# The end of a matmul-bound kernel: the last inner product in two half-width banks, and other ways out for the last block's quarters

## The chip, the core and the metric

The kernel runs on one core of one Trainium2 chip. The metric is the device time of one execution in microseconds. Float32 goes in and comes out, and all matrix products run in float32.

## The reference

```python
batch, n_heads, seq, head_dim = (4, 8, 768, 64)
mask = q_bucket[:, :, :, None] == k_bucket[:, :, None, :]      # 6 sign bits of q @ proj and of k @ proj
scores = scale * np.matmul(q, k.transpose(0, 1, 3, 2))
scores = np.where(mask, scores, -1000000000.0)
attn = softmax(scores)                                         # max, exp, divide by the sum + 1e-9
x = np.matmul(attn, v) as (B*S, H*D) = (3072, 512)
h = x @ w_in                                                   # 512 -> 2048
g = np.maximum(h, 0.0) ** 2
return g @ w_out                                               # 2048 -> 512, float32
```

## The kernel before

The kernel has two parts. Attention over the 32 heads, taken in pairs, fills the first 310 us or so and leaves x, transposed, in device memory. Then come three chunks of 1024 tokens each. A chunk goes through `hidden` or `hidden_pair` (x times `w_in`, then the squared ReLU) and then through `project` (times `w_out`), both with features on the partitions and tokens in the columns.

The matrix products are done with seven products of half-size blocks in place of eight, and `project` does this on two levels. Its outer loop runs over k = 0 to 6. For each k, `product` runs the inner seven: `add(to, a, b, first, last)` issues four matmuls of 128 x 128 weights and 256 columns (w = 256, n = 4) into the bank `acc[to]`. A float32 matmul stands in the trace as two passes, each with a weight load of its own, so one `add` shows as eight MATMUL and eight LDWEIGHTS records. Three banks are used. `acc[0]` is a running sum: ScalarE copies it out (`keep`) as `one`, `two` and `three` on its way, while later products add on to it. The four results, c11, c12, c21 and c22, go to VectorE (`add_to`, line 1306), which adds them up to blocks of the output.

The functions `first_` to `fourth` say what is done with the results of outer product k. The last one, k = 6, is `fourth`. It closes the block (ih, jh) = (1, 0), features 256 to 511 of the first 512 tokens of the chunk, in four quarters n = 0 to 3. Quarter n has row n // 2 (128 features) and column n % 2 (256 tokens). In the last chunk this is the last work of the kernel, and `product` is called there with `last`. The order in which the quarters close is then 0 (c11), 3 (c22), 1 (c12), 2 (c21). So "the second quarter" is n = 1, "the fourth quarter" n = 3, and the one that closes last is n = 2.

A quarter has features on its partitions and has to leave with tokens in the rows. There are two ways out:

- `put_part` (quarters 0, 3 and 1): VectorE transposes 32 x 32 blocks (line 1337), and four stores write 32 features each, 256 runs of 128 bytes (line 1341). `LATE` names the queue of each store: quarter 0 has three on GpSimd and one on SyncE, quarter 3 four on ScalarE, quarter 1 three on SyncE and one on ScalarE.
- `put_last` (quarter 2): TensorE transposes 128 x 128 (line 1356), VectorE copies the first half out of PSUM (line 1360), ScalarE the second (line 1358), and two stores write 128 runs of 512 bytes each (line 1361), the first on SyncE, the second on ScalarE.

Stores that `put_part` issues are listed in `late`. At the end, TensorE and VectorE each wait for `late[-1]` before they go on:

```python
for engine in nc.tensor, nc.vector:
    tc.add_manual_dep(engine.nop().ins, late[-1].ins.name, SYNC)
```

Behind that, every engine tests a flag (`tc.If`, line 1604) and branches past `general`, a slow path that is not taken with these inputs. Then SyncE waits in turn for every semaphore (line 1779), and two rounds of barriers end the kernel.

Instructions run on each engine in the order in which they are written. The framework gives each DMA of SyncE's and ScalarE's queues one of eight semaphores. A DMA is issued only when the DMA before it on the same semaphore has landed, and that wait stands on the issuing engine's queue. Tiles of one name share a few buffers: two each for the PSUM tiles `acc0`, `acc1` and `acc2`, five for the SBUF tiles `h` (`NH`), in which the transposed quarters are stored from.

Of the kernel before, what the change touches and what calls it, by code (L numbers as in the profile page):

```python
# [8 lines left out]
FP32 = mybir.dt.float32  # L9
# [25 lines left out]
def kernel(  # L35
# [10 lines left out]
    nc = tc.nc  # L46
# [6 lines left out]
    P = 128  # L53
# [12 lines left out]
    NCH = 1024  # L66
    NCHUNK = B * S // NCH
# [3 lines left out]
    ident = glob.tile([P, P], FP32, name="ident")  # L71
# [9 lines left out]
    HF, HD, NR, NQ = DFF // 2, DM // 2, NFF // 2, NFF // 4  # L81
# [623 lines left out]
    for pr in range(NIN, NP):  # L705
        n = 2 if pr % 2 else int(pr not in (NP // 2, NP - 2))
# [30 lines left out]
    with tc.manual_schedule():  # L737
# [180 lines left out]
        p_r = fast.enter_context(tc.tile_pool(name="p_r", bufs=2, reuse_waits="tile"))  # L918
        p_k = fast.enter_context(tc.tile_pool(name="p_k", bufs=1, reuse_waits="tile"))
        ps_m = fast.enter_context(tc.tile_pool(name="ps_m", bufs=2, space=PSUM, reuse_waits="tile"))  # L920
        HN, QN, NH = NCH // 2, NCH // 4, 5
# [6 lines left out]
        flags = []  # L928
        KEPT = dict(one=2, two=1, three=2, five=1)

        def product(n, w, at, bt, c11, c12, c21, c22, hook=None, last=False):

            acc = [ps_m.tile([P, 512], FP32, name=f"acc{i}")[:, 0:w] for i in range(3)]

            def add(to, a, b, first, last):
                for i in range(n):
                    nc.tensor.matmul(  # L940
                        out=acc[to], lhsT=a(i), rhs=b(i), start=first and i == 0,
                        stop=last and i == n - 1, skip_group_check=True,
                    )

            def keep(of, name):
                t = p_r.tile([P, 512], FP32, name=name, bufs=KEPT[name])[:, 0:w]
                nc.scalar.copy(out=t, in_=acc[of])  # L947
                return t

            add(0, at(0), bt["11"], True, False)  # L950
            one = keep(0, "one")
            add(1, at(1), bt["21"], True, True)
            if hook:
                hook()
            c11(acc[1], one)
            if last:
                flags.append(nc.values_load(slow))
            add(0, at(4), bt["t2"], False, False)
            two = keep(0, "two")
            add(2, at(3), bt["t1"], True, False)  # L960
            five = keep(2, "five")
            add(0, at(5), bt["t3"], False, False)
            three = keep(0, "three")
            add(2, at(6), bt["22"], False, True)
            if last:
                c22(three, five)
            c12(acc[2], two)
            if not last:
                c22(three, five)
            add(0, at(2), bt["t4"], False, True)  # L970
            c21(acc[0])

# [329 lines left out]
        def block(t, n):  # L1302
            return t[:, n]

        def add_to(out, one, two):
            nc.vector.tensor_tensor(out=out, in0=one, in1=two, op=ALU.add)  # L1306
# [20 lines left out]
                    in_=ot[a * 32:(a + 1) * 32].rearrange("i (c j) -> i c j", j=32),  # L1327
                )

        LATE = {0: (nc.gpsimd,) * 3 + (nc.sync,), 3: (nc.scalar,) * 4, 1: (nc.sync,) * 3 + (nc.scalar,)}  # L1330
        late = []

        def put_part(n, o):

            row, col = n // 2, n % 2
            ot = p_r.tile([P, HN], FP32, name="h", bufs=NH)[:, 0:QN]
            nc.vector.transpose(out=ot, in_=o)
            lo = (NCHUNK - 1) * NCH + col * QN
            m0 = HD + row * P
            for a in range(P // 32):  # L1340
                late.append(LATE[n][a].dma_start(
                    out=out[lo:lo + QN, m0 + a * 32:m0 + (a + 1) * 32].rearrange(
                        "(c i) j -> i c j", i=32
                    ),
                    in_=ot[a * 32:(a + 1) * 32].rearrange("i (c j) -> i c j", j=32),
                ))

        def put_last(n, o):

            row, col = n // 2, n % 2  # L1350
            ot = p_r.tile([P, HN], FP32, name="h", bufs=NH)[:, 0:QN]
            lo = (NCHUNK - 1) * NCH + col * QN
            for t in range(QN // P):
                at = slice(t * P, (t + 1) * P)
                tp = ps_m.tile([P, 512], FP32, name=f"acc{t}")[:, 0:P]
                nc.tensor.transpose(out=tp, in_=o[:, at], identity=ident)
                if t:
                    nc.scalar.copy(out=ot[:, at], in_=tp)
                else:
                    nc.vector.tensor_copy(out=ot[:, at], in_=tp)  # L1360
                (nc.scalar if t else nc.sync).dma_start(
                    out=out[lo + t * P:lo + (t + 1) * P, HD + row * P:HD + (row + 1) * P],
                    in_=ot[:, at],
                )

        def project(i):

# [11 lines left out]
            def close(ih, jh, n):  # L1379
                o = outs[ih, jh, n // 2]  # L1380
                o[1] += 1
                if (i, ih, jh) == (NCHUNK - 1, 1, 0):
                    put = put_last if n == 2 else put_part
                    put(n, o[0][:, n % 2 * QN:(n % 2 + 1) * QN])
                elif o[1] == 2:
                    put_out(i, ih, jh, n // 2, o[0])

# [31 lines left out]
            def fourth(n, one, two):  # L1419
                add_to(out_block(1, 0, n), block(W, n), whole(one, two))  # L1420
                close(1, 0, n)

            more = i + 1 < NCHUNK
            uses = first_, seventh, fifth, third, second, sixth, fourth
            for k in range(7):
                b = OUTER[k][1]
                t1, t2 = tens.pop(k)
                if k == 0 and more:
                    load_x(i + 1)
                src = load_factor_units(k - 1) if i == 0 and 0 < k <= NQ else None  # L1430
                if k == 1 and src:
                    factor_units(0, src)
                if k == 2 and more:
                    sum_x(i + 1, 1)
                    sum_x(i + 1, 2)
                if i == 0 and k == NQ + 1:
                    load_peak(0)
                    load_peak(1)
                if k >= 5 and more:
                    load_inner(i + 1, 0, (k - 5,))  # L1440
                at = lambda m, k=k: lambda n: leaves[k, m][:, n]
                bt = {
                    "11": lambda n: b[:, n, 0:QN], "21": lambda n: b[:, NQ + n, 0:QN],
                    "22": lambda n: b[:, NQ + n, QN:HN], "t1": lambda n: t1[:, n],
                    "t2": lambda n: t2[:, n], "t3": lambda n: b[:, n, QN:HN],
                    "t4": lambda n: b[:, NQ + n, 0:QN],
                }

                def hook():
                    y21 = b[:, NQ:NR, 0:QN]  # L1450
                    minus(y21, y21, t2)
                    if k > 1 and src:
                        factor_units(k - 1, src)
                    if k == 5 and more:
                        sums_inner(i + 1, (2,))
                    if k + 1 < 7 and k not in (1, 3):
                        inner_sums(k + 1)
                    if k == 6 and more:
                        load_third_inner(i + 1, 0, nc.scalar)
                        sums_inner(i + 1, (0, 1))  # L1460

                counted = []

                def a_with_load(m, k=k):
                    load_leaf(7 * k + len(counted) + NLEAF - 2)
                    counted.append(m)
                    return at(m)

                use = uses[k]
                product(  # L1470
                    NQ, QN, a_with_load, bt, lambda *p: use(0, *p), lambda *p: use(1, *p),
                    lambda p: use(2, p, None), lambda *p: use(3, *p), hook,
                    (i, k) == (NCHUNK - 1, 6),
                )
                if k == 3 and more:
                    sum_x(i + 1, 3)
                    sum_x(i + 1, 4)
                if k == 4 and i + 1 == NCHUNK:
                    guard()
                if k == 0:  # L1480

                    for h in range(2):
                        at_h = slice(h * NQ, (h + 1) * NQ)
                        minus(b11[:, at_h], b22[:, at_h], b_t[:, at_h])
                    inner_sums(2)
                if k == 2:

                    for h in range(2):
                        at_h = slice(h * NQ, (h + 1) * NQ)
                        minus(b_t[:, at_h], b21[:, at_h], b11[:, at_h])  # L1490
                    inner_sums(4)
# [43 lines left out]
        for i in range(NCHUNK):  # L1535
            for s in range(NR):
# [9 lines left out]
                if i == 0 and r in THEN:  # L1546
                    m = THEN.index(r)
# [15 lines left out]
                for n in range(2):  # L1563
                    m = 2 * ((i - 1) * NR + s) + n
# [218 lines left out]
```

## Time and profile before

| | |
|---|---|
| median of 3 runs | 853.48 us (853.28 to 853.53) |
| the profiled execution | 853.88 us; its span, first to last instruction, 852.3 us |
| TensorE busy | 845.8 us, 99% of the span, granted clock 0.999 |
| VectorE, ScalarE, GpSimd busy | 88%, 47%, 20% |
| last matmuls of the last inner product | end at 846.75 us |
| last store issued | SyncE, 848.32 us |

Times in the timeline are counted from the span's start. The span is the part of the execution between the first and the last instruction that the profiler recorded; the execution's own time has 1.5 us more around it. SPq and ACTq are the queues of SyncE and ScalarE as far as they issue DMAs. PE is TensorE's matmul, PEld its weight load, DVE VectorE, ACT ScalarE, POOL GpSimd. "q8" and "q14" of kind "instruction" are the queues that fetch the engines' own code.

### The profile page before, as it was taken

The numbers are of one execution on the slowest core, as the hardware profiler recorded it, in microseconds if no ns is written. First come the engines' busy times: TensorE is split into PE (matmuls) and PEld (weight loads), VectorE is DVE, ScalarE is ACT, GpSimd is POOL, SyncE is SP. The second block draws the span as 40 slices with busy tenths as digits, with TensorE's granted clock in tenths as the row PEclk, the third lists the DMA queues.
The fourth block names the chain that finished last, engine by engine and source line by source line (L and its number), as shares of the span: only waits on it lengthen the run. The fifth ranks groups of instructions, "written<-read, shape, count | busy, mean of one in ns | idle before, by whom it ended". The sixth has DMA issues, their size and how long they took to land.

```text
span 852.3 us, 17018 instructions
## 1 busy us (share of the span) xinstructions
PE 845.8 (99%) x6594; PEld 542.3 (64%) x6594; DVE 746.6 (88%) x1023; ACT 400.9 (47%) x749; POOL 168.4 (20%) x283
## 2 busy tenths in 40 slices
PE   9999999999999999999999999999999999999997
PEld 4475444444485444444788866567888756568886
DVE  4898999999999998988999968888988788889776
ACT  5787777878777762222111145553111355541110
POOL 1321121303221201543122121111000311200003
PEclk9999999999999999999999999999999999999999
DMA  9976998989995517999977975537557865335566
GB/s 214 175 130 138 183 187 202 212 167 227 266 233 184 183 43 272 324 319 304 354 227 234 271 194 188 188 95 296 178 161 195 180 221 189 124 118 148 158 162 140
DMA packets 234230, 170.14 MB, mean 200 GB/s; under 512 B 164841, under 2 KB 193329, under 8 KB 234145
## 3 DMA queue, kind: packets, MB, share of 16 engines
q1 hardware_dynamic: 194384, 87.78, 42.2%
q0 software_dynamic: 16512, 42.45, 15.7%
q10 hardware_dynamic: 23248, 38.78, 14.8%
q8 instruction: 53, 0.87, 0.4%
q14 instruction: 33, 0.26, 0.1%
HBM read 127.15 MB, written 41.16 MB: 197 GB/s over the span
## 4 chain that ended last, share of the span: by engine, by line
PE 97%; DVE 1%; DMA 1%; ACT 0%; issue 0%; SPq 0%; ACTq 0%; POOL 0%; DVEq 0%; POOLq 0%
PE acc L940 39%; PE st L478 18%; PE xo L532 15%; PE acc L1204 13%; PE acc L1157 9%; PE tot L589 1%; PE hash L396 1%; DMA out_dram<-h 1%; PE tp L342 0%; PE xo L371 0%; DVE h L1320 0%; DVE o L1306 0%; PE hash L406 0%; PE xo L406 0%; DVE tmp L1306 0%; DVE sum L1306 0%
## 5 line engine op out<-in xcount | busy, mean ns | idle before, releaser
L484 ACT ACTIVATE e<-st 128x768 f32<-128x768 f32 x192 | 155.4, 810 | 56.4 <-PE st L478 52.2
L532 PE MATMUL xo<-e,v_nat 64*64 64x385 f32 (+1 forms) x1520 | 158.4, 483 | 0.0
L940 PE MATMUL acc<-b,leaf 128*128 128x256 f32 x600 | 133.0, 379 | 0.0
L940 PEld LDWEIGHTS acc<-b,leaf 128*128 128x128 f32 x600 | 113.9, 190 | 16.0 <-issue 0.5
L478 PE MATMUL st<-feat 64*64 64x384 f32 x1056 | 110.0, 482 | 0.0
L532 PEld LDWEIGHTS xo<-e,v_nat 64*64 64x64 f32 (+1 forms) x1520 | 62.1, 133 | 62.1 <-issue 50.1
L444 POOL DMA_DIRECT2D bits<-signed x120 | 62.5, 525 | 195.7 <-ACT signed L433 193.9
L1204 PE MATMUL acc<-t_x,w_unit 128*128 128x512 f32 x192 | 90.8, 595 | 0.0
L940 PE MATMUL acc<-t,leaf 128*128 128x256 f32 x336 | 75.9, 379 | 0.0
L940 PEld LDWEIGHTS acc<-t,leaf 128*128 128x128 f32 x336 | 63.8, 190 | 8.7
L1017 DVE SCALAR_TENSOR_TENSOR b<-h 128x512 f32<-128x512 f32 x96 | 65.7, 691 | 3.0
L478 PE MATMUL st<-bits 64*64 64x384 bf16 x768 | 67.9, 324 | 0.0
L520 DVE TENSOR_TENSOR total<-total,e 128x1536 f32<-128x1536 f32 x32 | 56.0, 1749 | 4.8 <-ACT e L484 3.9
L520 DVE TENSOR_TENSOR t_x<-t_x,e 128x1536 f32<-128x1536 f32 x32 | 55.9, 1747 | 4.3 <-ACT e L484 4.2
L940 PE MATMUL acc<-x,w_unit 128*128 128x512 f32 x128 | 56.5, 593 | 0.0
L478 PEld LDWEIGHTS st<-feat 64*64 64x64 f32 x1056 | 40.5, 133 | 25.1 <-issue 21.1
L947 ACT COPY two<-acc 128x256 f32<-128x256 f32 (+1 forms) x29 | 12.5, 431 | 88.0 <-PE acc L940 66.1
L940 PE MATMUL acc<-b_t,leaf 128*128 128x256 f32 x240 | 53.8, 379 | 0.0
L1204 PEld LDWEIGHTS acc<-t_x,w_unit 128*128 128x128 f32 x192 | 35.8, 190 | 26.7 <-issue 23.0
L1325 POOL DMA_DIRECT2D out_dram<-h x24 | 15.5, 655 | 181.6 <-DVE h L1320 181.6
L478 PE MATMUL st<-t_x 64*64 64x384 f32 x480 | 50.0, 482 | 0.0
L940 PEld LDWEIGHTS acc<-b_t,leaf 128*128 128x128 f32 x240 | 45.6, 190 | 6.2
(192 smaller groups left out, 1346.3 us busy)
## 6 DMA issues: line engine op xcount, KB each, us to landing
leaf<-w_out ACTq DMA_DIRECT2D x142, 256.0 KB, 3.1
raw<-in_moe_w_in_dram SPq DMA_DIRECT2D x8, 1024.0 KB, 6.1
raw<-in_moe_w_out_dram SPq DMA_DIRECT2D x8, 1024.0 KB, 7.2
w_unit<-w_in SPq DMA_DIRECT2D x16, 512.0 KB, 4.0
w_unit<-w_in SPq DMA_DIRECT2D x8, 896.0 KB, 8.8
w_out<-sums POOLq DMA_DIRECT2D x16, 448.0 KB, 7.5
v_nat<-in_v_dram SPq DMA_DIRECT2D x16, 384.0 KB, 5.1
x_all<-x_raw SPq DMA_DIRECT2D x16, 384.0 KB, 3.2
```

The lines of the kernel that those rows point to most:

```text
L396: nc.tensor.matmul(out=banks[g * NR_B:(g + 1) * NR_B, h, 0:HS], lhsT=projs[rows, h * D:h * D + NR_B], rhs=feat[pr][rows, w, c * HS:(c + 1) ...
L444: nc.gpsimd.dma_start(out=t[h * D:h * D + NBITS + 1, w, c * HS:(c + 1) * HS], in_=signed[pr % 2][at:at + NBITS + 1, h],)
L478: nc.tensor.matmul(out=st[k * HK:(k + 1) * HK, h, 0:HS], lhsT=src[1][rows, key], rhs=src[0][rows, cut], start=first, stop=not first, skip_ ...
L484: nc.scalar.activation(out=key_of(pr, kt)[:, :, i, 0:HS], in_=st[:, :, 0:HS], func=ACTF.Exp, scale=scale)
L520: nc.vector.tensor_tensor(out=totals[pr], in0=totals[pr], in1=e, op=ALU.add)
L532: return nc.tensor.matmul(out=outs[pr][h * D:(h + 1) * D, c, 0:HS + 1], lhsT=nat[pr, "v_nat"][rows, h, kt * D:(kt + 1) * D], rhs=key_of(pr ...
L940: nc.tensor.matmul(out=acc[to], lhsT=a(i), rhs=b(i), start=first and i == 0, stop=last and i == n - 1, skip_group_check=True,)
L947: nc.scalar.copy(out=t, in_=acc[of])
L1017: nc.vector.scalar_tensor_tensor(out=out, in0=h, scalar=0.0, in1=h, op0=ALU.max, op1=ALU.mult)
L1157: nc.tensor.matmul(out=out, lhsT=w(a), rhs=b, start=start, stop=stop, skip_group_check=True)
L1204: nc.tensor.matmul(out=to, lhsT=w[:, PLACE[a], f], rhs=bt[b](f), start=first and f == 0, stop=last and f == NFT // 2 - 1, skip_group_check ...
L1325: queue.dma_start(out=out[at, m0 + a * 32:m0 + (a + 1) * 32].rearrange("(c i) j -> i c j", i=32), in_=ot[a * 32:(a + 1) * 32].rearrange("i ...
```

## The change

It has three parts, all in the last outer product of the last chunk.

1. The last inner product (`at(2)` times `t4`) no longer adds on to `acc[0]`. It goes in two groups of 128 columns into two banks of its own (`halves`), 16 passes of 128 columns in place of 8 of 256. `acc[0]` is added to the block as soon as it is complete without it, and each half is added in an instruction of 128 columns of its own.
2. Quarter 1 (the second) leaves as quarter 2 does: through two transposes of TensorE, two copies (ScalarE's for quarter 1, VectorE's for quarter 2) and two stores of 512-byte runs. The four stores of both quarters are issued behind all four copies: SyncE, ScalarE for quarter 1, ScalarE, SyncE for quarter 2.
3. The four stores of quarter 3 (the fourth) go in turn to ScalarE's queue and SyncE's. Quarter 1 is no longer in `late`, so `late[-1]` is now the last store of quarter 3.

```diff
-            add(0, at(5), bt["t3"], False, False)
+            add(0, at(5), bt["t3"], False, bool(last))
...
+            if last:
+                halves = [ps_m.tile([P, 512], FP32, name=f"acc{m}")[:, 0:w // 2] for m in range(2)]
+                a = at(2)
+                for m, half in enumerate(halves):
+                    for i in range(n):
+                        nc.tensor.matmul(
+                            out=half, lhsT=a(i), rhs=bt["t4"](i)[:, m * w // 2:(m + 1) * w // 2],
+                            start=i == 0, stop=i == n - 1,
+                        )
+                return last(acc[0], halves)
             add(0, at(2), bt["t4"], False, True)
             c21(acc[0])
...
-        LATE = {0: (nc.gpsimd,) * 3 + (nc.sync,), 3: (nc.scalar,) * 4, 1: (nc.sync,) * 3 + (nc.scalar,)}
+        LATE = {0: (nc.gpsimd,) * 3 + (nc.sync,), 3: (nc.scalar, nc.sync) * 2}
...
-        def put_last(n, o):
+        turned_last = []
+
+        def turn_out(n, o, t, ot, name, copy, queue):
...
+            at = slice(t * P, (t + 1) * P)
+            lo = (NCHUNK - 1) * NCH + col * QN + t * P
+            tp = ps_m.tile([P, 512], FP32, name=name)[:, 0:P]
+            nc.tensor.transpose(out=tp, in_=o[:, at], identity=ident)
+            copy(out=ot, in_=tp)
+            return lambda: queue.dma_start(
+                out=out[lo:lo + P, HD + row * P:HD + (row + 1) * P], in_=ot
+            )
...
-                    put = put_last if n == 2 else put_part
-                    put(n, o[0][:, n % 2 * QN:(n % 2 + 1) * QN])
+                    o = o[0][:, n % 2 * QN:(n % 2 + 1) * QN]
+                    if n in LATE:
+                        put_part(n, o)
+                    else:
+                        turned_last.append((n, o))
...
+            def finish(one, halves):
+
+                fourth(2, one, None)
+                (_, o1), (_, o2) = turned_last
+                for t, half in enumerate(halves):
+                    at = slice(t * P, (t + 1) * P)
+                    add_to(o2[:, at], o2[:, at], half)
+                ot = p_r.tile([P, HN], FP32, name="h", bufs=NH)
+                stores = []
+                for t in range(4):
+                    n, o, copy = ((1, o1, nc.scalar.copy), (2, o2, nc.vector.tensor_copy))[t // 2]
+                    stores.append(turn_out(
+                        n, o, t % 2, ot[:, t * P:(t + 1) * P], ("acc2", "acc2", "acc1", "acc0")[t],
+                        copy, nc.scalar if t in (1, 2) else nc.sync,
+                    ))
+                for store in stores:
+                    store()
...
-                    (i, k) == (NCHUNK - 1, 6),
+                    finish if (i, k) == (NCHUNK - 1, 6) else None,
```

## The prediction

> **What bounds the kernel now.** I read the page first, then the chain of waits, then the end of the timeline.
>
> ```profile
> PE 845.8 (99%) x6594; PEld 542.3 (64%) x6594; DVE 746.6 (88%) x1023; ACT 400.9 (47%) x749; POOL 168.4 (20%) x283
> PE 97%; DVE 1%; DMA 1%; ACT 0%; issue 0%; SPq 0%; ACTq 0%; POOL 0%; DVEq 0%; POOLq 0%
> ```
>
> TensorE is the bound for 97% of the chain. The diff touches nothing ahead of the last seven-product of the last project step, so only what lies behind TensorE's last matmuls can move. The timeline of the end (start us, us):
>
> ```profile
> 843.78 2.97 PE L940 MATMUL acc<-b_t,leaf 128*128 128x256 f32 x13
> ...
> 845.52 0.42 DVE L1306 TENSOR_TENSOR o<-sum,tmp 128x256 f32<-128x256 f32 x1
> 845.98 0.45 DVE L1337 STREAM_TRANSPOSE h<-o 128x256 f32<-128x256 f32 x1
> 846.79 0.42 DVE L1306 TENSOR_TENSOR o<-sum,acc 128x256 f32<-128x256 f32 x1 [0.36 <-PE acc L940]
> ...
> 847.63 0.29 DVE L1360 COPY h<-acc 128x128 f32<-128x128 f32 x1 [0.42 <-PE acc L1356]
> 847.74 0.27 ACT L1358 COPY h<-acc 128x128 f32<-128x128 f32 x1 [4.03 <-DMA out_dram<-h]
> 848.03 0.35 ACTq L1361 DMA_DIRECT2D out_dram<-h  x1
> 848.32 0.39 SPq L1361 DMA_DIRECT2D out_dram<-h  x1
> ```
>
> Matmuls end at 846.75, the last add (it was waiting for them) at 847.21, its copy on VectorE at 847.92. SyncE's store could follow at 847.97 but starts at 848.32: its queue still holds second-quarter stores. SyncE's own waits and the DMA rows of 849.0 to 851.5 say what follows:
>
> ```profile
> SPq L1779 <- DMA out_dram<-h: 1.4, 1, 1.4
> ...
> SPq L1341 <- DMA out_dram<-h: 0.6, 1, 0.6
> ```
>
> ```profile
> q14 instruction: 3, 0.02, 3.8%
> q8 instruction: 1, 0.02, 2.5%
> ```
>
> The kernel's end waits 1.4 us for one store. It is SyncE's last (L1361): "DMA to landing" gives 1.7 for ScalarE's and 2.7 for SyncE's, so 848.32 + 2.69 = 851.01. Its landing records come 15 within 849.78 to 849.95 and one at 851.01. In between, one queue's packets stand still from 849.56 to 850.13, exactly until an instruction fetch (8 KB, 849.53, 0.61 us) ends. Such fetches follow each engine's final branch: ScalarE's 848.41 to 849.53, VectorE's 848.79 to 850.01, TensorE's 848.79 to 850.44 (16 KB, 0.98 us). So a fetch holds one ring, and behind the release (850.13) the landing takes another 0.88. After that come 1.32 us of final waits and barriers: 852.33. The execution took 853.88, 1.55 beyond its span; the other runs' median is 853.48, 0.40 less, so I apply the difference to 853.48.
>
> **The change part by part.**
>
> *Narrow last group.* Removed: 8 passes of 256 columns (0.216 apart, 844.86 to 846.75). Added: 16 passes of 128 columns with 16 weight loads. A pass's length grows 595 - 379 = 216 ns for 256 more columns, so 128 columns take 0.108; a weight load grows 190 - 133 = 57 ns for 64 more columns, so its own streaming is 0.114. A load starts as the matmul ahead of it starts, so I take the larger: 0.114. Ends: 0.108 (free) and 0.216 (no shorter than now). The first half then ends at 844.86 + 7 x 0.114 + 0.27 (a 128-column pass, L997's 272 ns) = 845.93, the second at 844.86 + 15 x 0.114 + 0.27 = 846.84, 0.09 late. New banks mean no wait for earlier readers: both buffers' last readers are of the product before.
>
> *VectorE's row.* Removed: the second quarter's 32x32 transpose (0.45) and the wide add behind the last matmul. Added: the wide add of acc[0] now goes early, at 845.98 to 846.40, in the place of that transpose; then an add of 128 columns for each half. These have no row; ends 0.42 (the wide add) and 0.29 (the 128x128 copy); I take 0.29, nearest in size. First: 846.44 to 846.73. Second: it waits for 846.84, runs 846.88 to 847.17; behind it only two copies are queued. Now: 847.21. So this part gains 0.04; at 0.42 an add it loses 0.11 (both adds then run back to back to 847.32), at 0.108 a pass it gains 0.12.
>
> *Second quarter through TensorE.* Removed: four stores of 256 runs of 128 B, three on SyncE and one on ScalarE (issue 0.32 to 0.45 each). Added: two TensorE transposes behind the 16 passes (846.69, 0.11 apart, done 847.13; they delay the last quarter's, ready at 847.22, by nothing), two ScalarE copies of 0.27 (847.06 and 847.36; they wait for TensorE, and behind them ScalarE has only its own two stores queued), two stores of 128 runs of 512 B: SyncE at 847.37, ScalarE at 847.66.
>
> *Fourth quarter on two queues.* ScalarE now issues four from 845.14, the last at 846.54, with its fifth at 847.09 to 847.51. After: two each from 845.14, done by 846.0. That clears both queues. SyncE is free from 847.7 instead of 848.21, so its stall of 0.6 (L1341, for a landing at 847.39) and the 0.35 of queueing go.
>
> *Last quarter.* Last add 847.17, transpose, and VectorE's copies (same 0.42 behind the add) 847.22 and 847.59 to 847.88. SyncE's store 847.93, against 848.32: 0.39 earlier. ScalarE's second store stands behind its first: 847.66 + 0.35 + 0.04 = 848.05, against 848.03. This one is now the last to be issued: 0.27 earlier than SyncE's was.
>
> *Landing.* Ends: 1.72 (ScalarE's row, undisturbed) gives 849.77, 1.24 before 851.01; 2.69 (SyncE's row) gives 850.74. What decides is the fetches, and the change moves them: TensorE's and VectorE's final branches wait for the last store in `late`. That was the second quarter's on ScalarE (landed 848.76, so both branched at 848.79); now it is the fourth quarter's on SyncE, issued about 845.53, landing 1.6 to 2.25 later (rows of L1341), 847.1 to 847.8. So both branches come a microsecond earlier, and their fetches with them. With 2.25 (its nearest row is the store of 845.14, in the same crowd) VectorE's fetch starts at 847.78 + 1.22 = 849.0 and TensorE's at 847.78 + 1.65 = 849.43. The last store's packets run 0.72 to 1.36 behind its issue (ScalarE's row): 848.77 to 849.41. VectorE's fetch lies in it; TensorE's just misses. Held until 849.0 + 0.36 to 0.61, take 849.5, and landing 0.88 behind: 850.37. Nothing else of the span changes. **Sum: 851.01 - 850.37 = 0.64 earlier: 853.48 - 0.64 = 852.8.**
>
> **The rivals.**
>
> *No fetch meets it.* For it: a fetch holds one ring of 16 and only what that ring has not yet sent, and ScalarE's last store, sent by 849.39, met none. Against: two fetches now fall around the last packets, and the one store of before that was sent late was caught. Then 1.24 is gained, and up to 0.36 more if the last landing's semaphore is the last one in SyncE's row of final waits (seven of 0.06 follow it now): 852.2, at best 851.9.
>
> *TensorE's long fetch meets it.* If the gating store lands at 847.5 instead, that fetch runs from 849.15 to 850.13, the very moment of the release now: landing 851.01, and the earlier issue buys nothing. 853.5.
>
> *Slower: a narrow pass costs as much as a wide one.* For it: no row has a float32 pass shorter than its 190 ns weight load outside the transposes. Against: at 256 columns the pitch is all columns, and loads overlap. At 0.216 the second half ends 844.86 + 15 x 0.216 + 0.27 = 848.37 and the last store goes out at 849.46; with 1.72 to 2.69 it lands at 851.18 to 852.15, 0.2 to 1.1 late: 853.7 to 854.6. It decides from a pitch of about 0.16 on, where the second half is 0.7 late and eats my 0.64. The Trainium skill ("TensorE: Matmul & The Clock Gate", Back-to-back issue gap) speaks for a mild form: streams of load and matmul at 128 columns space 81 ns against 56 for the matmul alone. No row here shows such passes in float32. An estimate from the page's figures, 25 ns more per pass (0.133), puts the second half 0.3 later than mine and the sum at 853.1.
>
> That the narrow halves don't overlap with the adds as meant is in the forecast already: the first half's add is off the path.
>
> **How the numbers follow.** Forecast 0.45 (own range 852.3 to 853.2: the fetch's 0.36 or 0.61, the add's ends), no fetch 0.23, TensorE's fetch 0.2, slow pass 0.09, else 0.03. 0.2% is 1.7 us, about what a measurement of this kernel can tell from no change; so nearly all cases lie within. Faster by more needs the no-fetch case's far end and a short landing (1.54 is the shortest row): 0.1. Slower by more needs the slow pass and a held ring, or what I haven't seen: 0.05. Range 851.8 to 854.2: leaves out the best end (0.08), the slow pass's upper part (0.05) and the rest (0.03).
>
> **What would show it.** Right: 16 narrow passes 0.11 apart in the last group; SyncE without a wait for a landing ahead of its last store; last issue near 848.0; TensorE's and VectorE's branches near 847.8 and one landing record of a last store about 0.6 behind the other 15. Wrong: narrow passes 0.16 or more apart, a last landing at 849.8 (no fetch) or 851 (the long one), or anything ahead of 843 that moved.

## The result, and the profile after

| | before | after |
|---|---|---|
| median | 853.43 us (852.30 to 855.26, 22 runs) | 854.93 us (853.66 to 856.83, 22 runs) |
| ratio, 95% interval | | 1.0016 [1.0010, 1.0022] |
| the profiled execution | 853.88 us, span 852.3 | 854.51 us, span 853.0 |
| last inner product's matmuls end | 846.75 us | 847.14 us |
| last store issued | 848.32 us | 848.26 us |
| last store landed | 851.01 us | 851.92 us |
| end of the span, behind the last of those matmuls | +5.58 us | +5.82 us |

The change makes the kernel 1.4 us slower (0.16%; 0.9 to 1.9 by the interval), where 0.6 us earlier was forecast. The time lies above the forecast's range, though within 0.2% of before.

Executions differ in when they reach their end, by stages long before it that the change doesn't touch: the last product ended at 846.14 us in one profile below and at 848.66 in another. So I compare tails: what follows the last matmul of the last inner product (846.75 before, 847.14 after). "+4.8" below means that many us behind it.

The page's busy times and its chain of waits:

```profile
PE 846.4 (99%) x6604; PEld 529.3 (62%) x6604; DVE 746.8 (88%) x1025; ACT 401.3 (47%) x750; POOL 167.7 (20%) x283
...
PE 99%; ACT 0%; DVE 0%; issue 0%; POOL 0%; POOLq 0%
```

TensorE is still the whole of the chain; the change put ten matmuls in (6604 against 6594). This chain ends with VectorE's last copy (848.18) and leaves out the stores behind it. What the change can move lies in the last product and behind it, so the end of the timeline is what to read (start us, us, engine and line, what it does, in brackets idle time and what ended it):

```profile
844.98 1.97 PEld L975 LDWEIGHTS acc<-b_t,leaf 128*128 128x128 f32 x16
...
845.20 1.95 PE L975 MATMUL acc<-b_t,leaf 128*128 128x128 f32 x16
...
845.47 0.82 SPq L1351 DMA_DIRECT2D out_dram<-h  x2
845.47 0.89 ACTq L1351 DMA_DIRECT2D out_dram<-h  x2
...
846.20 0.41 DVE L1316 TENSOR_TENSOR o<-sum,acc 128x256 f32<-128x256 f32 x1
846.72 0.29 DVE L1316 TENSOR_TENSOR o<-o,acc 128x128 f32<-128x128 f32 x1
...
846.98 0.87 PE L1366 MATMUL acc<-ident,o 128*128 128x128 f32 x4
847.18 0.29 DVE L1316 TENSOR_TENSOR o<-o,acc 128x128 f32<-128x128 f32 x1 [0.18 <-PE acc L975]
847.29 0.43 ACT L1367 COPY h<-acc 128x128 f32<-128x128 f32 x2 [3.25 <-DMA out_dram<-h]
847.51 0.67 DVE L1367 COPY h<-acc 128x128 f32<-128x128 f32 x2
...
847.75 0.85 ACTq L1368 DMA_DIRECT2D out_dram<-h  x2
847.81 0.83 SPq L1368 DMA_DIRECT2D out_dram<-h  x2
```

Sixteen narrow passes take 1.95 us, 0.112 apart. The last add, 0.29 us, starts 0.04 behind the last pass's end. The two copies of the second quarter on ScalarE and the two of the last on VectorE follow, and then two stores leave on each queue, the last at 848.26. This execution reached the last product 0.33 us later than the one before (its add at 844.53 against 844.20). With that taken off, VectorE's row holds within 0.1 us of the forecast, and ScalarE's two stores leave 0.24 and 0.16 earlier, as its two copies take 0.43 together and not one after the other. The groups by shape give the passes' mean length (busy us, mean ns):

```profile
L975 PE MATMUL acc<-b_t,leaf 128*128 128x128 f32 x16 | 1.9, 275 | 0.0
L975 PEld LDWEIGHTS acc<-b_t,leaf 128*128 128x128 f32 x16 | 1.9, 192 | 0.1
```

The loss is behind the last issue. The views give fetches and landings only as sums and ranges; the times of single ones, here and below, are read from the trace's own packet and semaphore records. SyncE's own waits from 840 to 853, then the instruction queues in the DMA rows of 849.0 to 850.7 (packets, MB, share), then the times from issue to landing of the four last stores (L1368):

```profile
SPq L1806 <- DMA out_dram<-h: 2.2, 1, 2.2
SPq L1368 <- DMA out_dram<-h: 1.5, 1, 1.5
```

```profile
q14 instruction: 3, 0.02, 7.1%
q8 instruction: 1, 0.02, 5.3%
```

```profile
DMA to landing us min/median/max: 1.8/2.7/3.7
```

L1806 is the final wait (L1779 before): it now stands 2.2 us where it stood 1.4. The first two of the four stores landed 1.75 and 1.88 us behind their issue, the last two 3.54 and 3.66: at 851.76 and 851.92. Between them lie four code fetches. TensorE and VectorE took their final branches at 847.95 (848.79 before), and their fetches ran from 849.31 for 1.44 us (16 KB) and from 849.13 for 0.71 us (8 KB). ScalarE's and SyncE's ran from 849.74 on, 0.61 us each. A store leaves 16 landing records, taken here as one for each of the 16 rings that send its packets side by side. Of those of each late store 14 were in by 849.97 and 850.19, and the 15th came at 851.22 and 851.46, so more than one ring was held. The last packets of both ran from 850.75, just as TensorE's fetch ended, to 851.45. Before, 15 came together and one ring was late.

### The profile page after: what moved, and what is told of

Its sections match the earlier page's. It is cut to its first block, busy times and chain, and to the rows that moved or that the text cites. A ratio compares the mean times of both kernels' runs of the same rounds, so it can differ in the third digit from the quotient of the medians.

```text
span 853.0 us, 17041 instructions
## 1 busy us (share of the span) xinstructions
PE 846.4 (99%) x6604; PEld 529.3 (62%) x6604; DVE 746.8 (88%) x1025; ACT 401.3 (47%) x750; POOL 167.7 (20%) x283
## 4 chain that ended last, share of the span: by engine, by line
PE 99%; ACT 0%; DVE 0%; issue 0%; POOL 0%; POOLq 0%
PE acc L940 41%; PE st L478 18%; PE xo L532 15%; PE acc L1214 13%; PE acc L1167 9%; PE tot L589 1%; PE hash L396 1%; PE tp L342 0%; PE xo L371 0%; PE acc L975 0%; PE hash L406 0%; PE xo L406 0%; ACT e L484 0%; PE acc L1366 0%; DVE o L1316 0%
## 5 line engine op out<-in xcount | busy, mean ns | idle before, releaser
L532 PE MATMUL xo<-e,v_nat 64*64 64x385 f32 (+1 forms) x1520 | 155.0, 483 | 0.0
L478 PE MATMUL st<-feat 64*64 64x384 f32 x1056 | 107.6, 482 | 0.0
L532 PEld LDWEIGHTS xo<-e,v_nat 64*64 64x64 f32 (+1 forms) x1520 | 54.9, 133 | 69.3 <-issue 59.6
L478 PE MATMUL st<-bits 64*64 64x384 bf16 x768 | 64.2, 324 | 0.0
L478 PEld LDWEIGHTS st<-feat 64*64 64x64 f32 x1056 | 37.8, 133 | 27.7 <-issue 24.8
L940 PE MATMUL acc<-b_t,leaf 128*128 128x256 f32 x232 | 52.0, 379 | 0.0
L947 ACT COPY one<-acc 128x256 f32<-128x256 f32 (+1 forms) x29 | 12.5, 432 | 77.6 <-PE acc L940 53.4
```

Source lines behind the costliest of these rows:

```text
L478: nc.tensor.matmul(out=st[k * HK:(k + 1) * HK, h, 0:HS], lhsT=src[1][rows, key], rhs=src[0][rows, cut], start=first, stop=not first, skip_ ...
L532: return nc.tensor.matmul(out=outs[pr][h * D:(h + 1) * D, c, 0:HS + 1], lhsT=nat[pr, "v_nat"][rows, h, kt * D:(kt + 1) * D], rhs=key_of(pr ...
L940: nc.tensor.matmul(out=acc[to], lhsT=a(i), rhs=b(i), start=first and i == 0, stop=last and i == n - 1, skip_group_check=True,)
```

## The experiments

The theory after the result, A: the change lets TensorE and VectorE branch early, since `late[-1]` is now a store that lands early, and their fetches hold the rings under the last stores. The rivals. B: part 1 costs (sixteen passes, small adds). C: the stores themselves are slower as they now stand in a crowd of four. D: part 3 costs.

Ratios are each to the kernel before on the same chip, from 5 rounds; tails and landings are from one profile each. The change itself has 22 runs.

| | ratio, 95% | tail | last store(s) landed after issue, us |
|---|---|---|---|
| before, first profile | 1 | +5.58 | 2.69 |
| before, second profile (e8) | | +4.81 | 1.74, 1.85 |
| after | 1.0016 [1.0010, 1.0022] | +5.82 | 3.54, 3.66 |
| e1: after, TensorE and VectorE late | 0.9994 [0.9985, 1.0002] | +3.96 | 1.62 to 1.67 |
| e2: before, both early | 1.0018 [1.0009, 1.0027] | +6.05 | 3.29 |
| e3: after without part 1 | 1.0017 [1.0008, 1.0025] | +5.98 | 3.55, 3.62 |
| e4: before with part 3 | 1.0024 [1.0015, 1.0034] | +7.23 | 3.47 |
| e5: after without a branch | 0.9985 [0.9975, 0.9995] | +4.12 | 1.68 to 1.86 |
| e6: before, both later | 0.9998 [0.9989, 1.0007] | +4.57 | 1.59, 1.61 |
| e7: e1, first quarter on SyncE | 1.0023 [1.0014, 1.0032] | +7.22 | 3.59 |
| e9: after, only TensorE late | 1.0003 [0.9994, 1.0012] | +5.06 | 2.78, 2.96 |
| e10: after, only VectorE late | 1.0011 [1.0002, 1.0020] | +5.55 | 3.26, 3.34 |
| e11: e1 without part 3 | 0.9992 [0.9983, 1.0001] | +4.22 | 1.62 to 1.68 |
| e12: e1, ScalarE late too | 0.9989 [0.9980, 0.9998] | +3.94 | 1.59 to 1.66 |

### e1: the change, with the branches held back

```diff
                 for store in stores:
-                    store()
+                    turned_last.append(store())
...
-            tc.add_manual_dep(engine.nop().ins, late[-1].ins.name, SYNC)
+            tc.add_manual_dep(engine.nop().ins, turned_last[3].ins.name, SYNC)
```

`turned_last[3]` is the second quarter's store on ScalarE, one of the last four.

> The changed kernel with one edit: TensorE's and VectorE's final branches wait for quarter 1's ScalarE store (one of the last four) instead of quarter 3's last store. Theory A (the two branches come too early, and their instruction fetches hold rings while the last stores are under way): the branches move from 847.95 to about 849.5, their fetches to 850.6 and later, the last stores land about 1.75 after issue (near 850.0 instead of 851.9), the execution is 1.5 to 2 us shorter than the changed kernel, about 0.9985 of the kernel before. Theory B (the last stores are slow because four 64 KB stores and the two queues crowd each other, whatever the branches do): landing stays 3.5 us after issue, time stays at 1.0016 of before.

Measured: 853.26 us against 853.85, and all of the loss is gone. The gain over before that was expected, 0.9985, is only at the end of the interval. The landings of L1368, SyncE's waits from 840 on, and the DMA rows of 849.7 to 850.8:

```profile
DMA to landing us min/median/max: 1.6/1.6/1.7
```

```profile
SPq L1368 <- DMA out_dram<-h: 1.6, 1, 1.6
SPq L1806 <- PEq L1806: 0.7, 2, 0.5
```

```profile
q14 instruction: 1, 0.01, 3.8%
```

The final wait no longer names a store (no row L1806 <- DMA). TensorE's fetch (the row q8) is not in that stretch any more: the branch is at +2.29, its fetch at 851.31, when the last store had landed at 850.81. All three parts of the change are still in this kernel, so they cost nothing that shows: B, C and D fall as explanations of the loss.

### e2: the kernel before, with the branches early

```diff
-            tc.add_manual_dep(engine.nop().ins, late[-1].ins.name, SYNC)
+            tc.add_manual_dep(engine.nop().ins, late[4].ins.name, SYNC)
```

`late[4]` is the fourth quarter's first store. Nothing else of the change is in it.

> The kernel before with one edit: the two final branches wait for quarter 3's first store in place of quarter 1's last. Theory A: the branches move from 848.79 to about 847.7, TensorE's 16 KB fetch to about 849.3 and VectorE's to 848.9, into the packets of the last store (849.25 to 849.58); it lands 3 to 3.6 us after issue instead of 2.7, and the time is 1.001 to 1.002 of before, as the changed kernel's. Theory B: nothing else has changed, so 1.000.

Measured: 1.0018, as slow as the change. The landing of the two last stores (L1361) and the final wait (L1779):

```profile
DMA to landing us min/median/max: 3.3/3.3/3.3
```

```profile
SPq L1779 <- DMA out_dram<-h: 2.1, 2, 1.8
```

So the moved wait alone, without any of the new stores or passes, gives the whole loss. Together with e1 this shows that the wait is both needed and enough; that it acts through the fetches, as A says, is shown by e5.

### e3: the change without part 1

```diff
-            add(0, at(5), bt["t3"], False, bool(last))
+            add(0, at(5), bt["t3"], False, False)
...
-                halves = [ps_m.tile([P, 512], FP32, name=f"acc{m}")[:, 0:w // 2] for m in range(2)]
...
-                return last(acc[0], halves)
+                add(0, at(2), bt["t4"], False, True)
+                return last(acc[0], ())
```

> The changed kernel without its first part: the last inner product is one group of 256 columns added on to acc[0], and one wide add follows it. It tells what the narrow halves are worth by themselves. From the trace of the changed kernel (passes 0.112 apart, last add ended 847.47 against 847.21 plus the 0.33 by which that run was later) I expect the stores within 0.15 us of the changed kernel's and the time at 1.0016 of before (1.0008 to 1.0024). If the halves were what costs (theory C: more passes, adds and bank switches behind the matmuls), the time would go back to 1.000 or below.

Measured: 1.0017, no different from the change with its 1.0016. The landings of its four last stores are held in the same way:

```profile
DMA to landing us min/median/max: 1.6/2.6/3.6
```

### e4: the kernel before with part 3 alone

```diff
-        LATE = {0: (nc.gpsimd,) * 3 + (nc.sync,), 3: (nc.scalar,) * 4, 1: (nc.sync,) * 3 + (nc.scalar,)}
+        LATE = {0: (nc.gpsimd,) * 3 + (nc.sync,), 3: (nc.scalar, nc.sync) * 2, 1: (nc.sync,) * 3 + (nc.scalar,)}
```

> The kernel before with only the third part: quarter 3's four stores go in turn to ScalarE's and SyncE's queues; quarter 1 leaves as before, and the branches wait for its ScalarE store as before. Theory A: the branches come at that store's landing, which is now issued about 0.5 earlier (ScalarE has two stores less ahead of it), so fetches come a little earlier but the stores of SyncE do not: 0.999 to 1.001. Theory B (two queues at once crowd the rings): slower, 1.001 or more.

I missed this one: 1.0024, slower than before. That it is above the change's 1.0016 can't be told, as the intervals overlap. SyncE's waits of 840 to 853, and its row of the timeline:

```profile
SPq L1779 <- DMA out_dram<-h: 2.1, 1, 2.1
SPq L1341 <- DMA out_dram<-h: 1.8, 1, 1.8
```

```profile
842.76 6.33 SPq L1341 DMA_DIRECT2D out_dram<-h  x6
849.19 0.40 SPq L1361 DMA_DIRECT2D out_dram<-h  x1
```

SyncE's first store of the second quarter was ready at 846.45 and went out at 847.79. It stood behind a landing (847.73): that of the fourth quarter's first store on ScalarE, which had the same semaphore. In SyncE's queue everything behind it waited too, and the last store left at 849.19 (848.32 before). TensorE's branch in this kernel is at 848.28, so its fetch (850.06) and the others behind it then fell on that late store: 3.47 us to land. Part 3 by itself makes the kernel slower. In the change only one of the second quarter's stores is left on SyncE's queue; it waits for the same store's landing, but is ready only shortly ahead of it.

### e5: the change without the slow path

```diff
-    general(tc, flags[0], ident, w_in_7, w_in_21, w_out_1, q, k, v, proj, out)
```

The code of `general`, and with it the test of the flag and the branch, are left out.

> The changed kernel without the slow path behind the flag (these inputs never take it): no final branches, so no code fetched behind them, with TensorE's and VectorE's early wait left as it is. Theory A (the fetches behind the branches hold the last stores): no instruction packet after 847, the last stores land 1.6 to 1.9 after issue, 0.9 to 1.2 us less than the first-gate experiment's changed kernel end needs; from the last matmul of the last product to the span's end 3.3 to 4.0 us instead of 5.8, time 0.997 to 0.9985 of before. Theory D (it is the two engines' early end itself, or the power and clock state behind it, not the fetch): landing stays 3.5 after issue and the time near 1.0016 less the 0.5 of the branch.

Measured: 0.9985 (852.85 against 853.89). The DMA rows from 846 to 852 have no instruction queue; these are the two of the stores' queues, and the four last stores' landings:

```profile
q10 hardware_dynamic: 832, 0.20, 14.8%
q1 hardware_dynamic: 832, 0.20, 14.6%
```

```profile
DMA to landing us min/median/max: 1.7/1.7/1.9
```

Without fetches the landings are close to those of e1 (1.68 to 1.86 against 1.62 to 1.67), though TensorE and VectorE are through their wait as early as in the change (+0.48 and +0.76, against +0.80). So it is the fetches that hold the stores, and not the two engines' early end. The profile's tail, expected at +3.3 to +4.0, is +4.12 and not shorter than e1's +3.96, so what the ratio gains beyond e1 (0.0009, inside the intervals) isn't seen in the tail.

### e6 and e8: how much was there to gain?

e6 holds the branches of the kernel before back, up to its last store but one (`put_last`'s second, on ScalarE):

```diff
-                (nc.scalar if t else nc.sync).dma_start(
+                late.append((nc.scalar if t else nc.sync).dma_start(
...
-                )
+                ))
```

> The kernel before with the two final branches waiting for quarter 2's own ScalarE store, the last in its list, in place of quarter 1's. Theory A: the two fetches leave the last stores' time (from 850.0 and 850.4 to 851 and later), but in the trace of before it was ScalarE's fetch that held SyncE's last store, and that one stays; so a small gain, 0.9993 to 1.0002 of before. If time falls by as much as the same edit brought on the changed kernel (0.002), then TensorE's and VectorE's fetches cost as much there as well.

e8 is the kernel before, unchanged, profiled once more.

> The kernel before, unchanged, profiled once more, to see how far the end varies from execution to execution. From the last matmul of the last product to the span's end the first profile has 5.58 us, with 1.06 of it one ring's late landing. If that was chance, this one has 4.5 to 5.0; if it belongs to the kernel, 5.4 to 5.8 again.

Landings of the last two stores (L1361), e6 and then e8:

```profile
DMA to landing us min/median/max: 1.6/1.6/1.6
```

```profile
DMA to landing us min/median/max: 1.7/1.8/1.8
```

In e8 nothing is held, though nothing was changed. The fetch that held SyncE's store in the first profile, until 850.14, was ScalarE's: that engine's branch was at +1.66 and its fetch at +2.77, against +1.98 and +3.17 in e8. So the held landing of 2.69 us on which the forecast rests belongs to that execution, and not to every one; how often it comes, two profiles can't tell. e6 holds back only TensorE's and VectorE's branches, and leaves ScalarE's where it is (in its profile that fetch came no earlier than +3.04 and held nothing). Its 0.9998 says that the two fetches cost the kernel before nothing that 11 runs can tell. Between e6 (+4.57) and e1 (+3.96), two profiles with no fetch in the way, lies what the change's own three parts gain: 0.6 us by profiles, 0.0004 by ratios, whose intervals overlap.

### e7: the first quarter on SyncE

```diff
-        LATE = {0: (nc.gpsimd,) * 3 + (nc.sync,), 3: (nc.scalar, nc.sync) * 2}
+        LATE = {0: (nc.sync,) * 4, 3: (nc.scalar, nc.sync) * 2}
```

with e1's edits. GpSimd issues no store at the end.

> The changed kernel with the late gate (branches wait for quarter 1's ScalarE store) and quarter 0's four stores all on SyncE, none on GpSimd. In the late-gate experiment SyncE's store of quarter 1 waited 0.2 to 0.4 us for the landing of a quarter 3 store of the same semaphore, which GpSimd's branch fetch (8 KB, 0.6 us) had held for 0.65. With eight SyncE and ScalarE stores between, each of the last four reuses a semaphore of quarter 0, landed long before, and GpSimd's branch comes 1 us earlier. I expect SyncE's last store 0.2 to 0.3 earlier, the end at +3.7 behind the last matmul in place of +3.96, and 0.9990 to 0.9998 of before; slower than the late gate alone if the seven stores on one queue run into each other.

Missed as well: 1.0023. SyncE's wait and its rows of the timeline:

```profile
SPq L1351 <- DMA out_dram<-h: 2.6, 1, 2.6
```

```profile
843.59 5.80 SPq L1351 DMA_DIRECT2D out_dram<-h  x6
849.50 0.89 SPq L1368 DMA_DIRECT2D out_dram<-h  x2
```

It is e4's mechanism again: a landing on the other queue. SyncE's fourth store of the first quarter had been given the semaphore of ScalarE's first store of the fourth quarter; it was written earlier, yet stood until 847.58 for that landing, and the last store left at 850.02. TensorE's fetch (851.26) then fell on that store: 3.59 us to land. So the semaphores aren't dealt in the order in which the kernel writes the stores; by which order the framework deals them, no run here tests. What GpSimd's stores cost at the end stays open.

### e9, e10: which fetch?

```diff
-        for engine in nc.tensor, nc.vector:
-            tc.add_manual_dep(engine.nop().ins, late[-1].ins.name, SYNC)
+        for engine, store in ((nc.tensor, turned_last[3]), (nc.vector, late[-1])):
+            tc.add_manual_dep(engine.nop().ins, store.ins.name, SYNC)
```

This is e9, only TensorE late, on top of e1's first edit; e10 has the two stores exchanged.

> The changed kernel with only TensorE's final branch waiting for quarter 1's ScalarE store; VectorE's still waits for quarter 3's last store and branches early. It tells whose fetch holds the stores. Theory A1 (TensorE's 16 KB fetch, 1.0 to 1.7 us long, does the harm): time near the late gate's, 0.9992 to 1.0002 of before, last landing 1.7 to 2.2 after issue. Theory A2 (any early fetch holds a ring, the two add up): VectorE's 8 KB fetch of 0.3 to 0.8 us still costs about a third, 1.0002 to 1.001, landing 2.2 to 2.8 after issue.

> The reverse: only VectorE's final branch waits for quarter 1's ScalarE store, TensorE's branches early. Theory A1: as slow as the changed kernel, 1.0012 to 1.0022 of before, last landing 3 to 3.6 after issue. Theory A2: half way, 1.0005 to 1.0012.

Landings of the four last stores, e9 and then e10:

```profile
DMA to landing us min/median/max: 1.8/2.3/3.0
```

```profile
DMA to landing us min/median/max: 1.6/2.5/3.3
```

Against e1's slowest landing, 1.67, VectorE's early branch, with 8 KB to fetch, adds 1.3 us (e9), TensorE's, with 16 KB, 1.7 (e10), and both together 2.0 (after). By these profiles each is enough to hold the last stores, TensorE's holds them longer, and the two together cost less than their sum; in after's profile the two fetches overlap from 849.31 to 849.84. The figures are not those of one fetch alone: ScalarE's and SyncE's fetches follow close behind it (850.67 to 851.54 in e9, 851.24 to 852.07 in e10) and lie under the same late stores. The ratios have the same order (1.0003, 1.0011, 1.0016), their neighbours' intervals overlapping, and e9's does not exclude no change.

### e11, e12: the change at its best

e11 is e1 with `3: (nc.scalar,) * 4` in `LATE`, so without part 3. e12 is e1 with a third engine in the loop over engines and stores (against the change):

```diff
-        for engine in nc.tensor, nc.vector:
-            tc.add_manual_dep(engine.nop().ins, late[-1].ins.name, SYNC)
+        for engine, store in ((nc.tensor, turned_last[3]), (nc.vector, turned_last[3]), (nc.scalar, turned_last[3])):
+            tc.add_manual_dep(engine.nop().ins, store.ins.name, SYNC)
```

> The changed kernel with the late gate and without its third part: quarter 3's four stores all on ScalarE, as before. With the fetches out of the way this tells what the two queues are worth. ScalarE is then busy issuing until about +0.1 after the last matmul, its two copies and stores come 0.1 to 0.4 later, SyncE's store of quarter 1 reuses another semaphore. I expect 0 to 0.4 us more than the late gate alone: 0.9994 to 1.0002 of before. If the two queues were what made the landings late, this one would be the faster.

> The candidate for the fastest: the changed kernel with TensorE's, VectorE's and ScalarE's final branches all waiting for quarter 1's ScalarE store. In the late-gate experiment ScalarE's fetch began at 850.49, when three of the last four stores had just been sent; in the first profile of before it was this fetch that held SyncE's last store for a microsecond. Waiting costs ScalarE nothing as long as it is through its branch before SyncE's last final wait. I expect 0 to 0.3 us less than the late gate alone on average, 0.9988 to 0.9996 of before, and last landings of 1.6 to 1.9 after issue.

Measured: e11 0.9992, e12 0.9989. Landings of the four last stores of e12:

```profile
DMA to landing us min/median/max: 1.6/1.6/1.7
```

e11 and e1 can't be told apart, so part 3 is worth nothing here that can be measured. e12 has the lowest ratio of the kernels that keep the slow path: 853.42 us against 854.02 for the kernel before on the same chip, and its interval just excludes no change [0.9980, 0.9998]. It lies clear of the change's interval, but not of e1's and e11's, so what ScalarE's late branch adds is not shown.

## Why the prediction was wrong

**Narrow group: right.** 0.112 us a pass against 0.114, so the rival of slow passes is out. The estimate from the Trainium skill ("TensorE: Matmul & The Clock Gate", Back-to-back issue gap), 0.133 a pass, doesn't hold here: what loads add to 0.108 of columns is 0.004, not 0.025.

**VectorE's row: right.** Two adds of 0.29; the last ends 0.33 behind the last matmul, where 0.33 was forecast.

**Second and fourth quarter on the queues: half right.** The last issue is +1.11 behind the last matmul, against +1.56 before. In the forecast's terms, 848.05 against 846.84, it is +1.21, so even a little better. But "SyncE's stall of 0.6 goes" failed: the stall is 1.5 us now (L1368). SyncE's store waits for the landing (847.74) of a fourth-quarter store on ScalarE with the same semaphore. It went out at 847.81, only 0.11 later than the forecast's 847.37 shifted by the 0.33 us that this execution ran late, so the price was small by luck. In e4 and e7 the same mechanism cost the queue 1.3 and 2.6 us.

**Landing: the step that failed.** I had the mechanism (the branches move up with `late[-1]`, and fetches hold rings), the branch time (847.8 forecast; 847.95 less 0.33 is 847.62) and VectorE's fetch. Three things in the step were wrong (the forecast's clock is this execution's less 0.33):

- "TensorE's just misses." I took its start as 1.65 behind the branch and its length as 0.98, from one row. It came 1.36 behind and took 1.44. It started 0.45 earlier than forecast, ahead of the last two stores' packets, and ended at 850.75, in the forecast's clock 850.42, where I had the release at 849.5: 0.9 late. This is the second rival's mechanism, and nearly its condition: the gating store landed at 847.59 in the forecast's clock, where the rival had 847.5. e2 and e10 show it.
- The price of a hit. I took one ring and 0.88 us from release to landing. With four fetches on the rings it was 1.0 and 1.2, and the second rival's 853.5 was too low for that and for the next reason. Of this, the packets that the ring still had to send took 0.7 (850.75 to 851.45), against 0.15 in the profile before; what the rest is, no run shows.
- The base. The forecast subtracted from a landing of 851.01 that was itself held. The second profile of the kernel before (e8) had no hold and ended 0.77 sooner behind its last matmul. Against such an execution there was that much less to win, and a hit, which I priced as "buys nothing", is a loss.

By size: the span was forecast to end at 852.33 - 0.64 = 851.69 and ended, in the forecast's clock, at 852.63, 0.94 too late. The base was 0.77 too long if e8's tail is the usual one, which one profile doesn't show. Together these are 1.71 of the 2.14 us between the forecast 0.64 earlier and the medians' 1.50 later. The other 0.4 is not accounted for; two profiles of the kernel before differ by more.

**The first rival, no fetch,** did not happen, but e1 and e11 show what it would have been: 0.9994 and 0.9992, or 0.5 to 0.7 us with intervals that reach no change, where I had said 1.24. With the base of e8 instead of the first profile it comes out at 0.5.

**The range** failed with the base: all of its cases, the slow pass too, were counted from the held landing of 851.01.

## What to carry to other kernels

An engine's final branch was followed here by a fetch of its code that held rings under the kernel's last stores, so let the branches of engines that are done early wait for a store that goes out last, and when a store is taken off a list, look at who waits for that list's last entry. When stores move between queues, look up which of them share a semaphore: a store can stand for a landing of the other queue and hold its whole own queue. And where the gain to be had is a wait of about a microsecond in one profile, take a second profile of the kernel before to see whether it is there each time.

## What was unexpected in the hardware

- A fetch comes late and its length varies. It started 1.1 to 2.0 us behind the branch, 8 KB took 0.31 to 0.86 us and 16 KB 0.98 to 1.69 us over these profiles. It is TensorE that fetches 16 KB (in e9 and e10 that fetch moves with TensorE's branch), the others 8 KB. The Trainium skill ("Runtime: NRT & Kernel Launch", Instruction fetch mechanics) has blocks of 16 KiB, fetched by a DMA queue that the sequencer drives itself. Here queues for code alone are seen (q8 and q14), and the 16 KiB only for TensorE on q8; the other engines' fetches stand together under q14. It also says that a taken branch to a target outside the two pages at hand has to wait for the fetch of the target's page. Here the engine's next instruction came 0.5 us behind the branch, ahead of the fetch; whether the target lay outside, no run shows.
- One engine's early branch costs the last store 1.3 or 1.7 us beyond its usual 1.6 (e9, e10), more than that engine's fetch itself lasts (0.68 and 1.24 there); the other engines' fetches behind it have their part in this.
